# Attention weights stored per head, the seventh block of keys as one full product: 12 products per pair of heads and query range become 11

## The chip, the cores and the metric

The kernel runs on one core of a Trainium2 chip. The metric is the device time of one execution in microseconds. TensorE multiplies matrices, VectorE, ScalarE and GpSimd work on rows of up to 128 partitions, and SyncE issues the transfers (DMAs). In the profile they are PE (with PEld for its weight loads), DVE, ACT, POOL and SP.

## The reference

Two layers follow each other. The inputs are 8 batches, 12 heads, 448 rows and 64 columns per head.

```python
q_n, k_n = (rmsnorm(q, g_q), rmsnorm(k, g_k))
scores = scale * np.matmul(q_n, k_n.transpose(0, 1, 3, 2))
attn = np.exp(scores - np.max(scores, axis=-1, keepdims=True))
attn = attn / (np.sum(attn, axis=-1, keepdims=True) + 1e-09)
x = heads_side_by_side(np.matmul(attn, v))          # (8, 448, 768)
h = gelu(x @ w_in)                                  # (8, 448, 1024)
u, v = h[..., :512], h[..., 512:]
v_n = (v - mu) / np.sqrt(var + 1e-06) * g_ln
v_s = np.einsum('ts,bsd->btd', w_sg, v_n) + b_sg[None, :, None]
out = x + (u * v_s) @ w_out
```

`w_in` and `w_out` are float64 at the kernel's input and are decoded in the kernel.

## The kernel before

**Precision.** Most products are made from 16-bit floats: a number is split into a high part and a low part, and a product of two numbers is high x high + high x low + low x high. So attention times v is three products: `vh` with the high attention weights, `vl` with the high ones, and `vh` with the low ones.

**The work on attention.** A pair is two heads, a unit is two pairs (`NG = 2`); there are 48 pairs and 24 units. The 448 rows are taken as 7 groups of 64 (`C7 = 7`; row number p x 7 + c is place p of group c). For each of the 7 row blocks `t` of a unit, `scores` has 12 products of 64 rows by 64 columns for each of two heads; the output of one head holds 64 queries of each of the two pairs on its 128 partitions, and 448 keys in a row. VectorE takes the maximum (`jk`, `nm`), ScalarE the exponential `ex` with its sum, into 32-bit words `[P, 2, S]`. The 16-bit halves of these words serve as the attention weights: the upper half is the high part, the lower half, scaled by `UNIT`, the low part. They are written to `ahl` by two instructions (`scaled(ahl[:, 0], ...)` on ScalarE, `scaled(ahl[:, 1], ...)` on VectorE or ScalarE), 896 elements each: in `ahl` stand the high parts of head 0, of head 1, then the low parts of head 0, of head 1. One DMA transposes `ahl` in 14 blocks of 128 columns into `at`, so that keys come to the partitions.

448 keys are three and a half blocks of 128. So the fourth block of `at` has the last 64 keys of head 0 on its lower 64 partitions, and the first 64 of head 1 on its upper ones; the same holds for the low parts seven blocks later. v is laid out to match: per pair, `vr` holds for each head three blocks of 128 rows, and one 64-row group of each head shares a block. Four DMAs bring the v rows of three pairs.

```python
steps = [[(lo, CM), (hi, CM)]] + [[(slice(0, P), c), (slice(0, P), C4 + c)] for c in range(CM)]
blocks = [(v_, o, hx) for v_, o in (("vh", 0), ("vl", 0), ("vh", C7)) for hx in steps]
blocks = blocks[0::C4] + [x for m, x in enumerate(blocks) if m % C4]
```

`pv(u, e)` is called twice for a unit: e = 0 for four row blocks (256 columns a matmul), e = 1 for three (192 columns). With `steps` above, each of the three products has one step of 64 rows (`lo` for head 0, `hi` for head 1) and three of 128 rows, and each step is two matmuls, one for each head, side by side on 64 columns of the array each. The 64-row steps of both pairs come first. A call yields after step 5 and step 14 (`CUTS`), so that other work can come between its three pieces. Then VectorE multiplies by `row` (the reciprocal sums), ScalarE makes `xh` and VectorE `xl`, which the second layer (`moe`) reads.

**v.** `vsquares` sums the squares of three pairs' v on ScalarE, from which `vscale` makes one power of two for a batch; `vsplit` makes `vh` (ScalarE) and `vl` (VectorE), 448 elements a partition.

**The order.** Every operation is recorded on a tape with a cost by formula (`Tape.cost`), and `schedule` then writes the order of each engine as a list scheduler does: of what is ready, the lowest program number comes first, and an operation given to `either` goes to the engine that would end it first by the formula. TensorE tries to stay in one mode (128 or 64 rows, 128 or 64 columns), since a change of mode has a cost there. Because all is emitted in one place, nearly all instructions bear the line number L439 in the profile, and one is told from another by the tile names. Pools are rings: `at` has one buffer for each of its two ranges, `ahl` three, `vh` and `vl` four, `vr` two. SyncE issues all DMAs from one queue in the written order.

Of the kernel before, what the change touches and what calls it, by code (L numbers as in the profile page):

```python
# [46 lines left out]
NOT, NX, NEX = 2, 6, 2  # L47
EXP_SET = "natural_log_exp_and_others"
# [55 lines left out]
class Tape:  # L104
# [30 lines left out]
    def cost(self, q, op, a, kw):  # L135
# [15 lines left out]
        if q.eng != "S" and "dma" in op:  # L151
            return 700, 4000, None
# [48 lines left out]
    def record(self, q, op, a, kw):  # L201
# [12 lines left out]
        if q.eng == "S":  # L214
            t.preds |= self.after
# [231 lines left out]
def kernel(  # L447
# [76 lines left out]
    ENG = dict(A=A, V=V, G=G)  # L524

# [54 lines left out]
    def decode(dst, raw, most=None):  # L580
# [8 lines left out]
        V.scalar_tensor_tensor(out=di, in0=lo, scalar=29, in1=di, op0=ALU.logical_shift_right, op1=ALU.bitwise_or)  # L589

    def weights():
# [10 lines left out]
        def load_raw(j):  # L602
            if j < len(chunks):
# [3 lines left out]
                SP.dma_start(out=raws[j].rearrange("p a b -> p (a b)"),  # L607
# [5 lines left out]
        for x in (1, 0):  # L613
# [13 lines left out]
            for t in range(KT):  # L627
                wh, wl = (wi[:, t, x, n] for n in range(2))
                A.activation(out=wh, in_=dec[t], func=AF.Copy, scale=wsc)
                V.scalar_tensor_tensor(out=wl, in0=dec[t], scalar=wsc, in1=wh, op0=ALU.mult, op1=ALU.subtract)  # L630
# [33 lines left out]
        if PADS:  # L664
# [50 lines left out]
    def load_v(i):  # L715
# [6 lines left out]
        vr = ld.tile([P, GV, C7, D], F32, name="vr", bufs=NVR)  # L722
        vp = vr.rearrange("p g c d -> p g (c d)")
        src = v[b, 2 * g:2 * (g + GV)].rearrange("(g h) (p c) d -> h p g (c d)", h=2, c=C7)
        for h, half, s0, c0, n in ((0, lo, 0, 0, C4), (0, hi, 0, C4, CM), (1, lo, C4, C4, CM), (1, hi, CM, 0, C4)):
            SP.dma_start(out=vp[half, :, s0 * D:(s0 + n) * D], in_=src[h][:, :, c0 * D:(c0 + n) * D])
        for j in range(GV):
            VR[i + j] = vp[:, j]
# [48 lines left out]
    def vsquares(i):  # L777
# [6 lines left out]
        n = GV * C7 * D  # L784
# [12 lines left out]
    def vsplit(i):  # L797
        r = R.setdefault(i, {})
        sc = VS[i // NP]["sc"]
        vh, vl = (att.tile([P, C7, D], F16, name="v" + c, bufs=NVH) for c in "hl")  # L800
# [3 lines left out]
        V.scalar_tensor_tensor(out=vl.rearrange("p c d -> p (c d)"), in0=vr, scalar=sc, in1=vf, op0=ALU.mult, op1=ALU.subtract)  # L804
# [4 lines left out]
    def scores(u):  # L809
# [5 lines left out]
        for t in range(C7):  # L815
# [24 lines left out]
            scaled(ahl[:, 0], halves[:, :, :, 1], 1.0, HI)  # L840
            scaled(ahl[:, 1], halves[:, :, :, 0], UNIT, EL)
# [15 lines left out]
    def rows(e, rh, rl):  # L857
# [9 lines left out]
        row = att.tile([P, C4 * P], F32, name="row", bufs=1)[:, 0:n * P]  # L867
# [5 lines left out]
    def pv(u, e):  # L873
# [20 lines left out]
        V.tensor_tensor(out=ps, in0=ps, in1=row, op=ALU.mult)  # L894
# [5 lines left out]
        V.tensor_tensor(out=xl, in0=ps, in1=xh, op=ALU.subtract)  # L900
# [19 lines left out]
    def moe(b, early=False):  # L920
# [49 lines left out]
        def layernorm():  # L970
# [22 lines left out]
            for t in range(CK):  # L993
                s_ = tiles[t][1]
                V.tensor_scalar(out=vg[:, s_], in0=vg[:, s_], scalar1=mv[:, t, 0:1], scalar2=y[:, t:t + 1],
                                op0=ALU.subtract, op1=ALU.mult)
                copy(vh[:, s_], vg[:, s_], VH)
# [40 lines left out]
        for f in range(FT):  # L1038
            ps = ps_m.tile([P, 512], F32, name="ms_", tag="mm")
            n = 0  # L1040
            for t in range(CK):
                p0, p1, o, k = 0, P, t * DH + f * P, t
                if t == CM:
                    p0 = f // 2 * HP
                    p1, o = p0 + HP, t * DH + f % 2 * P
                    if PADS:
                        p0, p1, k = 0, P, CM + f // 2
# [201 lines left out]
```

## Time and profile before

| | |
|---|---|
| runs, us | 858.94, 857.5, 861.17 |
| profiled execution, us | 860.37 |
| its span, us | 858.6 |
| busy TensorE / ScalarE / VectorE / GpSimd, us | 743.0 / 722.3 / 668.2 / 304.5 |
| mean granted TensorE clock | 0.936 |
| matmuls `pv` / `s` | 2304 / 2016 |
| instructions `ahl` on ScalarE / VectorE | 192 / 144 |
| transposing DMAs `at` / `qt` | 168 / 48 |

The busy times are unions over the span. A row of a group gives its line, engine, operation, tiles out<-in, form, count, then busy time and mean duration, then the idle time of the engine before it and what ended that. In a row of the time order the numbers are the start in us and the length from the first start to the last end, xN the number of instructions merged. `64*64` ahead of a matmul's form says that it uses 64 rows and 64 columns of the array.

### The profile page before, as it was taken

What the parts mean: (1) busy time and instruction counts of PE and PEld (TensorE: products, weight loads), DVE (VectorE), ACT (ScalarE), POOL (GpSimd) and SP (SyncE); (2) the same over time, 40 slices, a digit from 0 to 9 for tenths busy, and PEclk for the clock granted to TensorE, in tenths of its full rate; (3) what the DMA queues carried; (4) which work ended last, traced back from release to release, by engine and by line L of the source; (5) the groups of instructions that cost most, each with busy time, mean ns of one, the idle gap of its engine ahead of it and who ended that gap; (6) DMA issues with size and microseconds to landing.
All of it is one profiled execution on the core that took longest, in us unless ns stands there. A gap on an engine that the chain in (4) does not pass through costs nothing.

```text
span 858.6 us, 21024 instructions
## 1 busy us (share of the span) xinstructions
PE 743.0 (87%) x7766; PEld 475.1 (55%) x7766; DVE 668.2 (78%) x1691; ACT 722.3 (84%) x1495; POOL 304.5 (35%) x457
## 2 busy tenths in 40 slices
PE   0445568954999979999999999999999999999997
PEld 0223343532675548655765568556855686558557
DVE  6978988889988878977976898878987978574250
ACT  4677879998898999898989999889999999895451
POOL 2543350045534634452444246323435335000000
PEclk9658668966999999999999999999999999999999
DMA  6999999969999998999699979997999699646002
GB/s 165 252 241 195 216 207 199 213 141 200 169 234 218 226 190 166 246 209 166 137 206 225 226 145 226 240 209 134 198 225 218 140 223 200 136 90 143 19 1 74
DMA packets 433944, 155.97 MB, mean 182 GB/s; under 512 B 402545, under 2 KB 427697, under 8 KB 433841
## 3 DMA queue, kind: packets, MB, share of 16 engines
q1 hardware_dynamic: 433840, 154.63, 89.6%
q8 instruction: 61, 1.00, 0.5%
q14 instruction: 43, 0.34, 0.1%
HBM read 43.57 MB, written 11.01 MB: 64 GB/s over the span
## 4 chain that ended last, share of the span: by engine, by line
PE 55%; ACT 17%; DVE 12%; DMA 9%; issue 5%; POOL 1%; SPq 1%; ACTq 0%; DVEq 0%; POOLq 0%
PE pv L439 11%; PE s L439 7%; DMA at<-ahl 6%; ACT ex L439 4%; ACT ahl L439 3%; DVE jk L439 2%; ACT L439 2%; ACT sqk L439 2%; PE row L439 1%; DVE ahl L439 1%; DMA qk<-in_k_dram 1%; ACT vg L439 1%; ACT u L439 1%; ACT vh L439 1%; DVE pv L439 1%
## 5 line engine op out<-in xcount | busy, mean ns | idle before, releaser
L439 DVE TENSOR_SCALAR_CACHE_REDUCE jk<-s 128x448 bf16<-128x448 f32 x336 | 199.0, 615 | 34.8 <-PE s L439 34.4
L439 ACT ACTIVATE ex<-s,nm 128x448 int32<-128x448 f32 x336 | 213.6, 641 | 12.1 <-DVE jk L439 9.8
L439 ACT ACTIVATE ahl<-ex 128x896 f16<-128x896 uint16 x192 | 181.9, 957 | 9.5 <-DMA at<-ahl 8.9
L439 PE MATMUL s<-qt 64*64 64x448 f16 x2016 | 142.8, 375 | 48.4 <-DMA qt<-hl 21.3
L439 PEld LDWEIGHTS <-vh 128*64 128x64 f16 (+2 forms) x1792 | 103.2, 112 | 103.6 <-issue 55.7
L439 PE MATMUL pv<-at,vh 128*64 128x192 f16 (+3 forms) x1536 | 133.0, 275 | 27.6 <-ACT ex L439 12.3
L439 DVE TENSOR_SCALAR ahl<-ex 128x896 f16<-128x896 uint16 x144 | 102.5, 712 | 28.8 <-ACT ex L439 22.7
L439 PEld LDWEIGHTS <-qt 64*64 64x64 f16 x2016 | 64.7, 110 | 94.4 <-issue 52.5
L439 POOL TENSOR_TENSOR hl<-qk,hl 128x896 f16<-128x896 f32 (+2 forms) x69 | 93.7, 1364 | 41.7 <-ACT hl L439 9.7
L439 PEld LDWEIGHTS <-wi 128*128 128x128 f16 x576 | 54.5, 99 | 55.5 <-issue 7.2
L439 POOL TENSOR_TENSOR qk<-qk,ny 128x896 f32<-128x896 f32 x46 | 77.1, 1690 | 14.5 <-DVE ahl L439 7.5
L439 POOL TENSOR_TENSOR qk<-qk,gg 128x896 f32<-128x896 f32 x23 | 48.1, 2093 | 96.0 <-ACT sqk L439 77.4
L439 PEld LDWEIGHTS <-xh 128*128 128x128 f16 (+1 forms) x648 | 49.7, 102 | 47.7 <-issue 20.8
L439 PE MATMUL pv<-at,vl 128*64 128x192 f16 (+3 forms) x768 | 74.0, 273 | 0.0
L439 ACT ACTIVATION_READ_ACCUMULATOR ex<-s,nm 128x1 f32 x336 | 71.6, 213 | 0.0
L439 POOL TENSOR_SCALAR rx<-sums 128x8 f32<-128x8 f32 (+1 forms) x48 | 15.0, 313 | 141.8 <-ACT ex L439 140.3
L439 PEld LDWEIGHTS <-vl 128*64 128x64 f16 (+2 forms) x896 | 56.1, 114 | 12.8 <-issue 0.7
L439 DVE TENSOR_REDUCE ss<-sqk 128x14 f32<-128x896 f32 x48 | 51.8, 1079 | 10.2 <-ACT sqk L439 10.1
L439 DVE TENSOR_TENSOR pv<-pv,row 128x512 f32<-128x512 f32 (+1 forms) x48 | 30.2, 629 | 34.3 <-PE pv L439 34.1
L439 ACT ACTIVATE sqk<-qk 128x896 f32<-128x896 f32 x48 | 45.8, 960 | 3.4 <-DMA qk<-in_k_dram 1.8
L439 PEld LDWEIGHTS <-xl 128*128 128x128 f16 (+1 forms) x408 | 36.6, 102 | 19.5 <-DVE v_i L439 1.1
L439 ACT ACTIVATE xh<-pv 128x512 f16<-128x512 f32 (+1 forms) x48 | 26.2, 547 | 24.4 <-DVE pv L439 23.7
(1104 smaller groups left out, 1799.7 us busy)
## 6 DMA issues: line engine op xcount, KB each, us to landing
qk<-in_q_dram SPq DMA_DIRECT2D x48, 224.0 KB, 3.9
qk<-in_k_dram SPq DMA_DIRECT2D x48, 224.0 KB, 4.7
out_dram<-ot SPq DMA_DIRECT2D x56, 192.0 KB, 3.4
raw<-in_moe_w_in_dram SPq DMA_DIRECT2D x12, 512.0 KB, 5.4
vr<-in_v_dram SPq DMA_DIRECT2D x32, 192.0 KB, 4.2
vr<-in_v_dram SPq DMA_DIRECT2D x32, 144.0 KB, 3.7
rawo<-in_moe_w_out_dram SPq DMA_DIRECT2D x8, 384.0 KB, 3.6
at<-ahl SPq DMA_TRANSPOSE x168, 4.6
```

What stands on the lines that cost most here:

```text
L439: ins = getattr(q.nc_eng, op)(*first, *a, **kw)
```

## The change

Attention weights are written per head: in `ahl`, and so in `at`, head 0 has its seven blocks, then head 1. Within a head come the 448 high parts, then the low parts of the last 64 keys, then the low parts of the first 384. So the fourth block of a head has the high parts of the last 64 keys on the lower 64 partitions, and their low parts on the upper ones. v's last 64 rows stand twice in `vr`, on the lower and on the upper partitions, so that one product of 128 rows with `vh` gives high x high and high x low for these keys, and one with `vl` gives low x high (and low x low, which was not computed before). A pair has 3 x 3 steps for the first 384 keys and 2 for the last 64: 11, all of 128 rows, in place of 9 of 128 and 3 of 64. `blocks` is now in the order of pair, then product; the cuts stay after steps 5 and 14, of 22 steps in place of 24. The low parts are written by two instructions, of 768 and 128 elements. `vr`, `vh`, `vl` have 512 elements a partition in place of 448; the squares count the last rows twice, in a scale that only has to be some power of two. v is loaded by three DMAs for three pairs.

```diff
-        vr = ld.tile([P, GV, C7, D], F32, name="vr", bufs=NVR)
-        vp = vr.rearrange("p g c d -> p g (c d)")
-        src = v[b, 2 * g:2 * (g + GV)].rearrange("(g h) (p c) d -> h p g (c d)", h=2, c=C7)
-        for h, half, s0, c0, n in ((0, lo, 0, 0, C4), (0, hi, 0, C4, CM), (1, lo, C4, C4, CM), (1, hi, CM, 0, C4)):
-            SP.dma_start(out=vp[half, :, s0 * D:(s0 + n) * D], in_=src[h][:, :, c0 * D:(c0 + n) * D])
+        vr = ld.tile([P, GV, 2 * C4, D], F32, name="vr", bufs=NVR)
+        vp = vr.rearrange("p g (h c) d -> p (g h) (c d)", h=2)
+        src = v[b, 2 * g:2 * (g + GV)].rearrange("h (p c) d -> p h (c d)", c=C7)
+        for half, s0, c0, n in ((lo, 0, 0, C4), (hi, 0, C4, CM), (hi, CM, CM, 1)):
+            LD[VQ].dma_start(out=vp[half, :, s0 * D:(s0 + n) * D], in_=src[:, :, c0 * D:(c0 + n) * D])
...
-        n = GV * C7 * D
+        n = GV * 2 * C4 * D
...
-        vh, vl = (att.tile([P, C7, D], F16, name="v" + c, bufs=NVH) for c in "hl")
+        vh, vl = (att.tile([P, 2 * C4, D], F16, name="v" + c, bufs=NVH) for c in "hl")
...
-            scaled(ahl[:, 0], halves[:, :, :, 1], 1.0, HI)
-            scaled(ahl[:, 1], halves[:, :, :, 0], UNIT, EL)
+            parts = ahl.rearrange("p x h n -> p (x h n)").rearrange("p (h n) -> p h n", h=2)
+            scaled(parts[:, :, 0:S], halves[:, :, :, 1], 1.0, HI)
+            scaled(parts[:, :, CK * P:C7 * P], halves[:, :, 0:SM, 0], UNIT, EL)
+            scaled(parts[:, :, S:CK * P], halves[:, :, SM:S, 0], UNIT, TL)
...
-        steps = [[(lo, CM), (hi, CM)]] + [[(slice(0, P), c), (slice(0, P), C4 + c)] for c in range(CM)]
-        blocks = [(v_, o, hx) for v_, o in (("vh", 0), ("vl", 0), ("vh", C7)) for hx in steps]
-        blocks = blocks[0::C4] + [x for m, x in enumerate(blocks) if m % C4]
+        blocks = [(v_, m, m + o) for v_, o in (("vh", 0), ("vl", 0), ("vh", CK)) for m in range(CM)]
+        blocks += [("vh", CM, CM), ("vl", CM, CM)]
...
-        steps = [(j, x) for part in (blocks[:3], blocks[3:]) for j in range(NG) for x in part]
-        for k_, (j, (v_, o, hx)) in enumerate(steps):
-            for h, (ks, c) in enumerate(hx):
-                mm(out=pc[h * HP:(h + 1) * HP, j], lhsT=R[NG * u + j][v_][ks, c], rhs=av[ks, o + c, j, 0:n],
+        steps = [(j, x) for j in range(NG) for x in blocks]
+        for k_, (j, (v_, m, o)) in enumerate(steps):
+            for h in range(2):
+                mm(out=pc[h * HP:(h + 1) * HP, j], lhsT=R[NG * u + j][v_][:, h * C4 + m], rhs=av[:, h * C7 + o, j, 0:n],
                    start=(k_ == 0), stop=(k_ == len(steps) - 1), skip_group_check=True)
```

`TL` is 'VA' as `EL` is, so VectorE or ScalarE. The rest of the diff adds switches (`STK`, `DEC`, `XL`, `VL`, `WL` and the queues' `RQ` to `XQ`) whose values leave the program as it was: all DMAs stay on SyncE's queue, and the operations on their engines.

On TensorE, here is the start of the first piece of a call with 192 columns near the middle of the program (the tile `at_7512` before, its counterpart `at_7476` now):

```order
L439 MATMUL ms__7767<-ws_h,vl 128x448
L439 LDWEIGHTS vh
L439 MATMUL pv<-at_7512,vh 64x3x64
L439 LDWEIGHTS vh
L439 MATMUL pv<-at_7512,vh 64x3x64
L439 LDWEIGHTS vl
L439 MATMUL pv<-at_7512,vl 64x3x64
```
```order
L443 LDWEIGHTS rl
L443 MATMUL row<-ident_h,rl 64x128
L443 LDWEIGHTS vh
L443 MATMUL pv<-at_7476,vh 64x3x64
L443 LDWEIGHTS vh
L443 MATMUL pv<-at_7476,vh 64x3x64
L443 LDWEIGHTS vh
L443 MATMUL pv<-at_7476,vh 64x3x64
```

Before, this piece is the 64-row steps of both pairs, `vh` and `vl` in turn, and score products in the same mode follow it; now it is the first six 128-row steps of the first pair, and it follows the products of `row`, which have the same mode. The third piece of a call has 14 matmuls in place of 18.

On VectorE, these are the rows ahead of the thirteenth unit's first multiplication by `row`:

```order
L439 SCALAR_TENSOR_TENSOR vl<-vr,v_s,vh 128x448 x2
L439 TENSOR_SCALAR ahl<-ex 128x896
L439 TENSOR_SCALAR jk,nm<-s 128x448 x2
L439 RECIPROCAL ry<-rx 128x6
L439 TENSOR_SCALAR jk,nm<-s 128x448 x2
L439 TENSOR_TENSOR pv<-pv,row 128x512
```
```order
L443 TENSOR_SCALAR ahl<-ex 128x2x384
L443 TENSOR_SCALAR ahl<-ex 128x2x64
L443 RECIPROCAL ry<-rx 128x6
L443 TENSOR_SCALAR ahl<-ex 128x2x384
L443 TENSOR_SCALAR ahl<-ex 128x2x64
L443 TENSOR_TENSOR pv<-pv,row 128x512
```

The one copy of 896 elements has become two, which mostly follow each other, and the maxima (`jk`) of this place now stand elsewhere.

On SyncE's queue, this is the load of v for three pairs, in the second half of the program:

```order
L439 DMA vr<-in_v_dram 64x3x256
L439 DMA vr<-in_v_dram 64x3x192 x2
L439 DMA vr<-in_v_dram 64x3x256
```
```order
L443 DMA vr<-in_v_dram 64x6x256
L443 DMA vr<-in_v_dram 64x6x192
L443 DMA vr<-in_v_dram 64x6x64
```

Four issues have become three, the last of which brings the repeated rows in pieces of 64 numbers.

More of the change, by code (lines that the diff above doesn't have):

```diff
@@ L539, in two, with stt @@
         tape.either(*[(ENG[e], "tensor_tensor", dict(out=out, in0=in0, in1=in1, op=op)) for e in on])
+    def stt(out, in0, by, in1, op0, op1, on):
+        tape.either(*[(ENG[e], "scalar_tensor_tensor", dict(out=out, in0=in0, scalar=by, in1=in1, op0=op0, op1=op1)) for e in on])
     SSW = 2 * C7
@@ L629, in weights @@
                 A.activation(out=wh, in_=dec[t], func=AF.Copy, scale=wsc)
-                V.scalar_tensor_tensor(out=wl, in0=dec[t], scalar=wsc, in1=wh, op0=ALU.mult, op1=ALU.subtract)
+                stt(wl, dec[t], wsc, wh, ALU.mult, ALU.subtract, WL)
                 if t % 2:
@@ L663, in weights @@
             yield
-        if PADS:
+        if PADS and not STK:
             for w_t in (ws_h, ws_l):
@@ L866, in rows @@
             return ps
-        row = att.tile([P, C4 * P], F32, name="row", bufs=1)[:, 0:n * P]
+        row = att.tile([P, C4 * P], F32, name="row", bufs=2 if "G" in XL else 1)[:, 0:n * P]
         scaled(row, ps, 2.0 ** -25, RW)
@@ L893, in pv @@
             row = rows(e, *r_)
-        V.tensor_tensor(out=ps, in0=ps, in1=row, op=ALU.mult)
+        if "G" in XL:
+            sx = att.tile([P, C4 * P], F32, name="sx", tag="row", bufs=2)[:, 0:n * P]
+            V.tensor_tensor(out=sx, in0=ps, in1=row, op=ALU.mult)
+            ps = sx
+        else:
+            V.tensor_tensor(out=ps, in0=ps, in1=row, op=ALU.mult)
         if e == 0:
@@ L899, in pv @@
         copy(xh, ps, XH)
-        V.tensor_tensor(out=xl, in0=ps, in1=xh, op=ALU.subtract)
+        two(xl, ps, xh, ALU.subtract, XL)
         if e == 1:
@@ L992, in layernorm @@
             vl = mlp.tile([P, CM * DH + FH], F16, name="vl")
-            for t in range(CK):
+            for t in (CM, *range(CM)) if STK else range(CK):
                 s_ = tiles[t][1]
@@ L996, in layernorm @@
                                 op0=ALU.subtract, op1=ALU.mult)
+                if STK and t == CM:
+                    vs = mlp.tile([P, 2, FH], F16, name="vs")
+                    for x, (own, far) in enumerate(((lo, hi), (hi, lo))):
+                        copy(vs[own, x], vg[own, s_], VH)
+                        V.tensor_tensor(out=vl[own, s_], in0=vg[own, s_], in1=vs[own, x], op=ALU.subtract)
+                        SP.dma_start(out=vs[far, x], in_=vl[own, s_])
+                    V2["vs"] = vs
+                    continue
                 copy(vh[:, s_], vg[:, s_], VH)
@@ L1047, in moe @@
                         p0, p1, k = 0, P, CM + f // 2
+                if STK and t == CM:
+                    for wx in (ws_h, ws_l):
+                        mm(out=ps[:, 0:S], lhsT=V2["vs"][:, f // 2, f % 2 * P:(f % 2 + 1) * P], rhs=wx[:, CM], start=False, stop=(wx is ws_l))
+                    continue
                 for vx, wx in ((vh, ws_h), (vh, ws_l), (vl, ws_h)):
```

25 lines of the change are left out of this document (15 added, 10 removed).

## The prediction

> **What bounds the kernel now.** I read the windows by stage first, then the chain of waits by stage, then single rows. The times of the runs are 857.5 to 861.17 with the median 858.94; the profiled execution took 860.37, of which the span below is the part that the engines show, with 1.8 us around it.
>
> ```profile
> span 858.6 us, 21024 instructions
> ```
> ```profile
> core 0: us, PE busy (x) PEld busy (x) DVE busy (x) ACT busy (x) POOL busy (x), PEclk, DMA share, GB/s
> 0.00:240.00 240.00, 140.59 (x1440) 82.74 (x1440) 205.59 (x506) 193.35 (x384) 92.07 (x133) 0.78 0.95 201
> 240.00:780.00 540.00, 528.47 (x5759) 340.33 (x5758) 442.17 (x1137) 497.50 (x1057) 210.43 (x317) 1.00 0.98 192
> 780.00:859.00 79.00, 73.94 (x570) 52.06 (x569) 20.39 (x48) 31.48 (x56) 2.02 (x8) 0.99 0.23 53
> ```
> ```profile
> 660.00:720.00 60.00, 59.47 (x660) 42.97 (x659) 49.38 (x131) 56.93 (x125) 27.12 (x40) 1.00 0.91 180
> ```
>
> There are three stages. Up to 240 us the weights are decoded and TensorE has a granted clock of 0.78 and much idle time; VectorE is the fullest engine (205.59 of 240, 86%). From 240 to 780 TensorE is busy for 98% at the full clock, with ScalarE close behind (497.50 of 540, 92.1%) and VectorE at 82%. After 780 TensorE is nearly alone. The 60 us from 660 show that ScalarE can be at 94.9% (56.93 of 60) while TensorE still runs through.
>
> ```profile
> by line: DMA at<-ahl 13.2%; PE pv L439 10.4%; issue 8.4%; ACT ahl L439 7.6%; ACT ex L439 5.6%; DMA qk<-in_k_dram 4.0%; DVE jk L439 3.5%; ACT sqk L439 3.5%; DVE dec L439 3.1%; SPq L439 2.8%; ACT L439 2.7%; DMA qt<-hl 2.6%; PE s L439 2.5%; AC
> ...
> by line: PE pv L439 12.4%; PE s L439 9.8%; DMA at<-ahl 4.2%; issue 4.0%; ACT ex L439 4.0%; ACT L439 2.1%; ACT ahl L439 2.1%; PE row L439 1.8%; DVE jk L439 1.8%; DVE ahl L439 1.5%; ACT vg L439 1.4%; ACT u L439 1.1%; ACT vh L439 1.0%; ACT sqk
> ...
> by line: PE pv L439 6.6%; PE mv__13219 L439 5.2%; PE mv__13214 L439 5.1%; PE mv__13351 L439 5.1%; PE mu__13423 L439 4.3%; PE mu__13363 L439 4.3%; PE mu__13454 L439 4.3%; PE mu__13398 L439 4.3%; PE mo__13710 L439 3.5%; PE mo__13154 L439 3.4%
> ```
>
> These are the chains of the three stages in order. The products of attention with v (`pv`) are on the chain for 10.4% of 240, 12.4% of 540 and 6.6% of 79 us: 25.0 + 67.0 + 5.2 = 97.2 us. The instructions that make `ahl` are on it too: on ScalarE for 7.6% of 240 and 2.1% of 540, 29.5 us; on VectorE for 1.5% of 540, 8.1 us. The change makes the first cheaper and the second dearer.
>
> **TensorE.** A call of `pv` had 12 steps for each of 2 pairs, each step one matmul for either head; now it has 11. So 24 steps become 22, and the removed ones are of the 64-row kind: 6 of these go and 4 whole ones come. What matters is whether a 64-row step costs less than a whole one.
>
> ```profile
> 588.94 0.33 PE L439 MATMUL pv<-at,vh 64*64 64x192 f16 x4
> 589.10 0.24 PE L439 MATMUL pv<-at,vl 64*64 64x192 f16 x2
> 589.18 0.25 PE L439 MATMUL pv<-at,vh 64*64 64x192 f16 x2
> 589.36 0.36 PE L439 MATMUL ms__9495<-ws_h,vh 128*128 128x448 f16 x1
> ```
> ```profile
> 645.03 0.41 PE L439 MATMUL pv<-at,vl 128*64 128x192 f16 x6
> 645.27 0.41 PE L439 MATMUL pv<-at,vh 128*64 128x192 f16 x6
> ```
> ```profile
> 542.85 0.38 PE L439 MATMUL pv<-at,vh 64*64 64x256 f16 x4
> 543.07 0.27 PE L439 MATMUL pv<-at,vl 64*64 64x256 f16 x2
> ```
> ```profile
> 750.35 0.49 PE L439 MATMUL pv<-at,vl 128*64 128x256 f16 x6
> 750.68 0.49 PE L439 MATMUL pv<-at,vh 128*64 128x256 f16 x6
> ```
>
> From start to start, 4 matmuls of 64 rows take 0.16 us at 192 columns and 0.22 at 256, that is 0.08 and 0.11 for a step of two; 6 whole ones take 0.24 and 0.33, again 0.08 and 0.11. A half product costs as much as a whole one. The saving is two steps in a call: 2 x 0.11 + 2 x 0.08 = 0.38 us for the two calls of a unit, 9.1 us for 24 units at full clock, 6.8 for the 18 between 240 and 780. On the chain it is 1/12 of 97.2, **8.1 us**, and that is my term: 2.1 + 5.6 + 0.4 by stage.
>
> [...]
>
> A change of mode: 589.18 to 589.36 is 0.18 us where 0.08 was due, 0.10 for the change. The first six steps of a call could stand inside a run of score products in their own mode and no longer can, but the last two pieces always needed a change; over the whole written order I count 363 changes before and 367 now. That is 0.4 us, put at nothing.
>
> **The weights' copies.** For each of 168 row blocks ScalarE and VectorE copy the high and low halves of `ex` into `ahl`. Two instructions of 896 elements become three: 896 (the high halves, ScalarE), 768 and 128 (the low ones). In the new order the 768 stand on ScalarE 19 times and on VectorE 149 (before 24 and 144), the 128 on ScalarE 53 times and on VectorE 115.
>
> ```profile
> L439 ACT ACTIVATE ahl<-ex 128x896 f16<-128x896 uint16 x192 | 181.9, 957 | 9.5 <-DMA at<-ahl 8.9
> L439 DVE TENSOR_SCALAR ahl<-ex 128x896 f16<-128x896 uint16 x144 | 102.5, 712 | 28.8 <-ACT ex L439 22.7 <-DMA at<-ahl 5.5
> L439 ACT ACTIVATE row<-row 128x512 f32<-128x512 f32 x24 | 14.4, 600 | 2.0 <-PE row L439 2.0
> L439 ACT ACTIVATE row<-row 128x384 f32<-128x384 f32 x24 | 11.7, 488 | 0.0
> L439 ACT ACTIVATE ny<-nt 128x28 f32<-128x28 f32 x24 | 5.7, 237 | 0.2
> L439 DVE COPY xt<-xl 128x64 f16<-128x64 f16 x24 | 5.8, 243 | 0.0
> L439 ACT ACTIVATE vh<-vr,v_s 128x448 f16<-128x448 f32 x48 | 32.4, 676 | 7.1 <-PE pv L439 5.5 <-DVE v_s L439 1.4
> L439 DVE SCALAR_TENSOR_TENSOR vl<-vr,v_s,vh 128x448 f16<-128x448 f32 x48 | 36.1, 754 | 4.6 <-ACT vh L439 4.3
> L439 ACT ACTIVATE sqv<-vr 128x1344 bf16<-128x1344 f32 x16 | 21.4, 1337 | 3.2 <-issue 2.5 <-DMA vr<-in_v_dram 0.7
> ```
> ```profile
> L439 DVE TENSOR_SCALAR ahl<-ex x144: 593/624/2401, 30.1 to 786.1; 128x896 f16<-128x896 uint16 x144
> ```
>
> ScalarE: the two rows of `row` give 112 ns for 128 elements. 168 x 957 + 19 x (957 - 112 = 845) + 53 x 300 ns is 160.8 + 16.1 + 15.9 = 192.8 us against 192 x 957 = 183.7: **+9.1**. The 300 lie between 237 (28 elements) and 488 (384), nearer the first; the ends give +5.8 and +19.1. VectorE: the least time, 593 for 896 elements, and the 243 of a 64-element copy bracket the small one; a slope of 0.55 ns per element (from the least 593 down to that copy's least of 130 in its tile's rows below) gives 243 + 35 = 278 ns for 128 and 712 - 71 = 641 for 768. So 149 x 641 + 115 x 278 = 95.5 + 32.0 against 102.5: **+25.0**. With 130 to 712 for the small one it is +8 to +75. That two runs of 384 keep the rate of one run of 896 isn't shown for `ahl`; the copies of `hl`, which are cut in runs as well, have a least time of 346 for their smallest form of 384 elements, on the same slope.
>
> ```profile
> L439 DVE COPY xt<-xl x24: 130/174/1130, 136.8 to 722.1; 128x64 f16<-128x64 f16 x24
> ```
> ```profile
> L439 DVE CAST hl<-qk x33: 346/620/2097, 26.5 to 658.9; 128x384 f16<-128x384 f32 x14, 128x512 f16<-128x512 f32 x10, 128x896 f16<-128x896 f32 x9
> ```
>
> [...]
>
> v: its rows of a pair grow from 448 to 512 elements. `vh` adds at most 14% of 32.4, `vl` of 36.1, `sqv` of 21.4 (4.6, 5.1, 3.1), and with a fixed part as in `row` some 2.7, 3 and 2.7. Three copies of `hl` of 512 elements went from ScalarE to VectorE, at 600 ns as in `row` 1.8 us. Together ScalarE has +12.7 us and VectorE +30.
>
> ```profile
> core 0: us, DVE busy (x) ACT busy (x), PEclk, DMA share, GB/s
> 240.00:780.00 540.00, 82.18 (x118) 126.49 (x132) 1.00 0.98 192
> ```
>
> This window view of `ahl` alone has 250 of 336 instructions in the long stage, 74%: there ScalarE gets +9.4 (506.9) and VectorE +22 (464, 86%). VectorE's part has cover: it was idle for 98 us there, and 641 + 278 = 919 ns on VectorE lie beside the 957 of ScalarE's high half, so a block whose parts start together isn't later. Scaled by the shares on the chain, ScalarE's `ahl` adds 5% of 29.5 = 1.5 and VectorE's 24% of 8.1 = 2.0, of which I keep half for that cover. For v I add 0.7:
>
> ```profile
> vr<-in_v_dram SPq DMA_DIRECT2D x32, 192.0 KB, 4.2
> vr<-in_v_dram SPq DMA_DIRECT2D x32, 144.0 KB, 3.7
> ...
> qt<-hl SPq DMA_TRANSPOSE x48, 4.4
> ```
>
> a load of 672 KB in four DMAs becomes 768 KB in three; 14% of the 4.2 to landing is 0.6, once where a load is late, the rest is loaded one batch ahead. SP's queue gets 16 issues fewer, and the transposes behind them stay as many and as large; each waits for three copies now.
>
> Sum: -8.1 + 1.5 + 1.0 + 0.7 = **-4.9 us**, 855.5 against this execution, **854.0 against the median**. With nothing hidden the additions on the chain are 4.2 and it is -3.9; with all hidden -8.1.
>
> **Rivals**, in terms of the median. *ScalarE becomes the bound* (slower): at its present share of 92.1% its 506.9 us need 550 us in the long stage, 10 more, and with 0.4 gained at the end the time is 868.5; at the best stretch's 94.9% they need 534, 6 less, which is the forecast's gain. It decides from 506.9 / 540 = 93.9%: if ScalarE can't be held above that, the change loses. For it: the ScalarE instructions come in an order that waits for VectorE's maxima; against: the stretch at 660. *The additions take back what TensorE gives* (no difference): if the small copy on VectorE costs as much as the large one does on average, 712, VectorE's term on the chain is 73% of 8.1 = 5.9 and the sum is 0: about 859. *The half products were half price after all*: 12 steps were worth 10.5, 11 are 5% more, +4.6 + 3.2 and 867; the rows speak against it.
>
> **How the numbers follow.** Forecast 0.62, ScalarE as the bound 0.20, no difference 0.15, half price 0.03. The whole order is written anew, and waits shift both ways; I take a third of the 4.0% of 540 that the chain calls issue, 7 us, for that. The range begins at 854 - 3.2 (all additions hidden) - 7 = 843 and ends at 867, with the half-price case, short of ScalarE's full 868.5; about one case in ten is left out above and one below. Half a per cent, 4.3 us, is what a measurement tells from no change; the forecast lies just beyond it, so of its 0.62 I count 0.45 as faster and 0.17 as the same. The same has 0.17 + 0.15 + 0.03 (a mild case of ScalarE) = 0.35, slower 0.17 + 0.03 = 0.20.
>
> **What would show it.** In the changed profile: 2112 `pv` matmuls, all 128*64, at 0.08 and 0.11 a step; the 128-element `ahl` near 280 ns on VectorE and 300 on ScalarE, the 768 near 640; ScalarE busy about 735 us in all; the `pv` share of the chain down by 8. If instead the stage from 240 is as long as before with idle TensorE ended by ScalarE or by the transposes, the first rival is right. The forecast is wrong if the small copies cost 0.5 us or more, or if runs of 384 lose VectorE's rate.

## The result, and the profile after

The changed kernel takes **871.39 us** (median of 6 runs, 868.0 to 875.2) against 859.64 us (857.5 to 862.03) for the kernel before, measured beside it: a ratio of 1.0138, with a 95% interval of 1.0103 to 1.0173. It is slower by 11.8 us, where 4.9 us less were forecast and the range ended at 867. Three executions of the runs below that took 1266.1, 1456.9 and 3938.7 us are left out of every median and ratio.

```profile
span 868.9 us, 20822 instructions
```

The windows of the changed kernel by the same three stages:

```profile
core 0: us, PE busy (x) PEld busy (x) DVE busy (x) ACT busy (x) POOL busy (x), PEclk, DMA share, GB/s
0.00:240.00 240.00, 139.27 (x1425) 82.33 (x1426) 210.56 (x545) 200.53 (x416) 96.96 (x138) 0.81 1.00 212
240.00:780.00 540.00, 511.65 (x5470) 320.81 (x5469) 442.24 (x1192) 490.08 (x1048) 210.69 (x308) 1.00 0.97 187
780.00:869.00 89.00, 84.21 (x683) 59.72 (x680) 30.61 (x78) 41.36 (x79) 2.54 (x11) 1.00 0.26 63
```

TensorE has less to do (735.1 us in all, 743.0 before), but between 240 and 780 us it is idle for 28.4 us (540 less 511.65) where it was for 11.5 (540 less 528.47), and more is left for later: 84.21 us in the last window against 73.94. ScalarE isn't fuller: 490.08 of 540 us, 90.8% against 92.1%. VectorE has the same 442 us as before. Of the engines that compute, none has taken TensorE's place as the fullest of this stage. The DMA engines show a higher share than TensorE's 94.8%, 0.97 now and 0.98 before. That share alone is no sign of the loss: from 240 us to the end the changed kernel has 0.87 as given, and with set a below it has 0.92 there and takes 860.0 us. No run takes load off the DMA engines.

The groups by form for the operations that the change made or lengthened; the last numbers are the busy time and the mean in ns, then the idle time ahead of them:

```profile
L443 ACT ACTIVATE ahl<-ex 128x896 f16<-128x896 uint16 x168 | 160.5, 957 | 5.3 <-DMA at<-ahl 5.1
...
L443 DVE TENSOR_SCALAR ahl<-ex 128x768 f16<-128x768 uint16 x149 | 97.1, 652 | 28.7 <-ACT ex L443 21.9 <-DMA at<-ahl 5.3 <-ACT row L443 0.8
...
L443 DVE SCALAR_TENSOR_TENSOR vl<-vr,v_s,vh 128x512 f16<-128x512 f32 x48 | 41.4, 864 | 5.9 <-ACT vh L443 5.9
...
L443 ACT ACTIVATE vh<-vr,v_s 128x512 f16<-128x512 f32 x48 | 34.9, 726 | 6.8 <-DVE v_s L443 3.7 <-PE pv L443 3.0
L443 DVE TENSOR_SCALAR ahl<-ex 128x128 f16<-128x128 uint16 x115 | 29.6, 257 | 2.2 <-DMA at<-ahl 2.2
...
L443 ACT ACTIVATE sqv<-vr 128x1536 bf16<-128x1536 f32 x16 | 23.9, 1493 | 2.1 <-issue 1.3 <-DMA vr<-in_v_dram 0.8
...
L443 ACT ACTIVATE ahl<-ex 128x128 f16<-128x128 uint16 x53 | 16.3, 307 | 0.4
L443 ACT ACTIVATE ahl<-ex 128x768 f16<-128x768 uint16 x19 | 16.0, 843 | 3.5 <-DMA at<-ahl 3.3
```

And products of attention with v, in the order of time:

```profile
642.24 0.63 PE L443 MATMUL pv<-at,vh 128*64 128x256 f16 x8
642.71 0.28 PE L443 MATMUL pv<-at,vl 128*64 128x256 f16 x2
642.81 0.49 PE L443 MATMUL pv<-at,vh 128*64 128x256 f16 x6
643.14 0.28 PE L443 MATMUL pv<-at,vl 128*64 128x256 f16 x2
```
```profile
549.52 0.52 PE L443 MATMUL pv<-at,vh 128*64 128x256 f16 x6 [1.21 <-DMA at<-ahl]
549.87 0.49 PE L443 MATMUL pv<-at,vl 128*64 128x256 f16 x6
```
```profile
650.14 0.44 PE L443 MATMUL pv<-at,vh 128*64 128x192 f16 x6
650.41 0.41 PE L443 MATMUL pv<-at,vl 128*64 128x192 f16 x6
```

All products use 128 rows. At 256 columns a step of two takes 0.10 us from start to start (642.71 to 642.81), and three steps 0.33 (642.81 to 643.14) to 0.35 us (549.52 to 549.87, behind a wait for a transposing DMA). At 192 columns three steps take 0.27 us here (650.14 to 650.41) and 0.24 in another place (593.49 to 593.73). So a step costs about what it cost. The copies cost about what was forecast (below). The prices of single operations thus explain nothing of the loss.

The chain of waits in the long stage:

```profile
by line: DMA at<-ahl 8.5%; PE pv L443 8.3%; issue 7.5%; PE s L443 6.3%; ACT ex L443 4.2%; POOL qk L443 3.3%; ACT L443 3.2%; ACT ahl L443 3.1%; DVE jk L443 2.8%; DVE ahl L443 2.0%; ACT vg L443 1.9%; PE row L443 1.7%; ACT u L443 1.5%; DVE hl 
```

The products' share fell from 12.4% to 8.3%, but the transposing DMAs of the weights rose from 4.2% to 8.5% and "issue" from 4.0% to 7.5%. The chain is more often outside TensorE. What TensorE itself waited for from 240 us to the end, longest in total first (total, times, longest), of the kernel before:

```profile
engine line waited for: us in total, times, longest us
PE ms__4409 L439 <- DVE xl L439: 4.8, 1, 4.8
PE pv L439 <- DMA at<-ahl: 1.1, 2, 0.6
PE s L439 <- ACT row L439: 1.1, 1, 1.1
```

and of the changed kernel:

```profile
PE pv L443 <- DMA at<-ahl: 6.2, 5, 2.7
PE pv L443 <- ACT ex L443: 2.6, 2, 1.9
PE row L443 <- DVE xl L443: 2.5, 2, 2.2
PE ms__4477 L443 <- ACT ex L443: 2.4, 1, 2.4
PE mo__7985 L443 <- DVE gtl L443: 1.8, 1, 1.8
```

There is no single new wait. The largest row, the transposes of the weights, has grown by 5.1 us and stands for five places. Summed over all rows of this view, ScalarE ended 12.7 us of TensorE's idle time where it ended 2.6, VectorE 8.6 for 6.7, and the transposes 6.2 for 1.1.

The loss builds up slowly. The first multiplication by `row` on VectorE in a unit starts, in the changed kernel and the kernel before, at 197.56 and 215.24 us in the fifth unit, 243.59 and 244.12 in the sixth, 368.62 and 366.60 in the tenth, 584.62 and 579.53 in the seventeenth, 803.35 and 792.83 in the last. A lead of 17.7 us is nearly gone one unit later, and from the tenth unit on the changed kernel is behind. Such a picture calls for the question of whether the work or its order did it.

### The profile page after: what moved, and what is told of

The parts are those of the page before. It is cut to its first block, busy times and chain, and to the rows that moved or that the text cites. A ratio compares the mean times of both kernels' runs of the same rounds, so it can differ in the third digit from the quotient of the medians.

```text
span 868.9 us, 20822 instructions
## 1 busy us (share of the span) xinstructions
PE 735.1 (85%) x7574; PEld 462.9 (53%) x7574; DVE 683.4 (79%) x1814; ACT 732.0 (84%) x1540; POOL 310.2 (36%) x457
## 4 chain that ended last, share of the span: by engine, by line
PE 41%; ACT 15%; DVE 9%; DMA 6%; issue 6%; POOL 4%; SPq 0%; POOLq 0%; ACTq 0%; DVEq 0%
PE pv L443 7%; DMA at<-ahl 5%; PE s L443 4%; ACT ex L443 4%; ACT ahl L443 2%; ACT L443 2%; POOL qk L443 2%; DVE jk L443 2%; PE row L443 1%; DVE ahl L443 1%; ACT u L443 1%; ACT vg L443 1%; DMA vr<-in_v_dram 1%; ACT sqk L443 1%; DVE vl L443 1%
## 5 line engine op out<-in xcount | busy, mean ns | idle before, releaser
L443 ACT ACTIVATE ahl<-ex 128x896 f16<-128x896 uint16 (+2 forms) x240 | 186.2, 804 | 9.2 <-DMA at<-ahl 8.4
L443 PE MATMUL s<-qt 64*64 64x448 f16 x2016 | 133.7, 377 | 54.7 <-DMA qt<-hl 28.1
L443 DVE TENSOR_SCALAR ahl<-ex 128x768 f16<-128x768 uint16 (+1 forms) x264 | 118.9, 480 | 30.9 <-ACT ex L443 21.9
L443 PEld LDWEIGHTS <-vh 128*64 128x64 f16 (+1 forms) x1600 | 93.0, 113 | 85.9 <-issue 38.9
L443 PE MATMUL pv<-at,vh 128*64 128x256 f16 (+1 forms) x1344 | 102.9, 276 | 28.6 <-DMA at<-ahl 25.3
L443 PEld LDWEIGHTS <-qt 64*64 64x64 f16 x2016 | 54.6, 110 | 109.1 <-issue 57.8
L443 POOL TENSOR_SCALAR rx<-sums 128x8 f32<-128x8 f32 (+1 forms) x48 | 21.2, 442 | 192.7 <-ACT ex L443 191.3
L443 PE MATMUL pv<-at,vl 128*64 128x256 f16 (+1 forms) x768 | 81.2, 275 | 0.0
L443 PEld LDWEIGHTS <-xh 128*128 128x128 f16 (+1 forms) x648 | 50.1, 102 | 49.8 <-issue 24.2
L443 PEld LDWEIGHTS <-vl 128*64 128x64 f16 (+1 forms) x896 | 55.0, 114 | 27.0 <-issue 11.7
L443 DVE TENSOR_TENSOR pv<-pv,row 128x512 f32<-128x512 f32 (+1 forms) x48 | 30.2, 628 | 27.2 <-PE pv L443 27.0
L443 PE MATMUL row<-ident_h,rh 128*64 128x128 f16 x336 | 27.0, 232 | 25.0 <-POOL rh L443 19.0
```

Of the source, the lines that this page charges most:

```text
L443: ins = getattr(q.nc_eng, op)(*first, *a, **kw)
```

## The experiments

Three theories were tested. **A**: the third copy per row block, or ScalarE's added work in general, is on the path. **B**: the 22 whole products in their new places cost TensorE time that the 24 did not. **C**: the planner writes the whole program's order anew from costs and due times, any such new order moves the time by about as much as was seen, and the changed work itself costs little. The ratio of each run is against the kernel before, run beside it on the same chip; the medians of that kernel were 861.17 to 862.01 us there. A ratio is the better comparison between two runs of this list.

### Taking the third copy away, and adding it to the kernel before

The changed kernel with its low parts in one copy of 896 elements:

```diff
-            scaled(parts[:, :, CK * P:C7 * P], halves[:, :, 0:SM, 0], UNIT, EL)
-            scaled(parts[:, :, S:CK * P], halves[:, :, SM:S, 0], UNIT, TL)
+            scaled(parts[:, :, S:C7 * P], halves[:, :, :, 0], UNIT, EL)
```


> The changed kernel with the low parts of ahl written by one instruction of 896 elements in their natural order (so low parts meet the wrong rows of v; nothing else is left out). Theory A, the third copy: its 16 us on ScalarE and 30 us on VectorE are what lengthens the program, so without it the time falls from 871 to 850-857, below the kernel before by TensorE's saving. Theory B, the products: eleven whole steps in one order fit worse between the score products, so the time stays at 867-873. Theory C, the written order: a schedule written anew comes out better or worse by about 1% whatever is in it, so anything from 855 to 875 without regard to the copy.

Measured: 866.36 us, 1.008 [1.0053, 1.0107]. And the kernel before with the third copy:

```diff
-            scaled(ahl[:, 1], halves[:, :, :, 0], UNIT, EL)
+            scaled(ahl[:, 1, :, 0:SM], halves[:, :, 0:SM, 0], UNIT, EL)
+            scaled(ahl[:, 1, :, SM:S], halves[:, :, SM:S, 0], UNIT, EL)
```


> The kernel before with only the low parts' copy cut into 768 and 128 elements; products and v as before. Theory A: 859 plus 8 to 12, 867-872. Theory B: 859 within 0.5%. Theory C: anywhere within 1% of 859 to 862.

Measured: 859.53 us, 0.9978 [0.9961, 0.9995]. The groups by form of this kernel show that it does have the same added instructions:

```profile
L439 DVE TENSOR_SCALAR ahl<-ex 128x768 f16<-128x768 uint16 x144 | 91.3, 634 | 31.8 <-ACT ex L439 29.8 <-DMA at<-ahl 1.3
...
L439 DVE TENSOR_SCALAR ahl<-ex 128x128 f16<-128x128 uint16 x116 | 30.2, 260 | 0.0
...
L439 ACT ACTIVATE ahl<-ex 128x128 f16<-128x128 uint16 x52 | 16.2, 311 | 0.3
```

The kernel before takes 168 more copies and isn't slower. So the third copy isn't a cost that shows wherever it is put. Either run also has a new order, so neither is the price of the copy alone, and what the first of them gained by taking it away can't be laid to that price.

### The third copy on other engines

```diff
-TL = 'VA'
+TL = 'V'
```


> The changed kernel with all 168 small copies on VectorE. ScalarE loses 53 x 0.307 = 16 us, VectorE gets 53 x 0.257 = 14. Theory A in the form that ScalarE's idle time stays: 871 - 12 = 857-861. Theory A in the form that VectorE's or the block's latency counts: 871-880. Theory B: 871.

Measured: 863.61 us, 1.0031 [1.0012, 1.0051]. VectorE gets all 168 small copies, and the kernel is 8 us faster than as given. With `TL = 'G'`, on GpSimd:

> The changed kernel with all 168 small copies on GpSimd, which is busy for 36%: ScalarE loses 16 us, VectorE 30, GpSimd gets 168 x about 0.55 = 90. Theory A: 850-860, as with two copies, unless GpSimd's lateness delays the transposes, then 865-880. Theory B: 871.

Measured: 873.8 us, 1.0148 [1.0133, 1.0164]. In the groups by form the small copy costs 675 ns there; the 0.55 us expected was the author's estimate, which no run shows:

```profile
L443 POOL TENSOR_SCALAR ahl<-ex 128x128 f16<-128x128 uint16 x168 | 113.4, 675 | 262.0 <-DVE ahl L443 102.4 <-ACT ex L443 95.4 <-DMA at<-ahl 14.0
```

GpSimd is busy for 416.5 us instead of 310.2 and the time is that of the changed kernel as given. ScalarE has 722.7 us of work with the copy on VectorE and 726.8 with it on GpSimd, against 732.0. The first run fits A, if ScalarE were the path; the second does so only if GpSimd's slower copy took the gain away. The next pair tests the path.

### Less work for ScalarE

The squares of v that set its scale are taken of one pair in three, in the changed kernel

```diff
-        n = GV * 2 * C4 * D
+        n = 2 * C4 * D
```


> The changed kernel with the squares of v summed over one pair of three only (the scale comes out as another power of two): ScalarE has 16 x about 1.0 = 16 us less to do, spread over the program. Theory A2, ScalarE is the bound and its idle time (136 us in the kernel before, 137 in the changed one) is a constant of the program: 871 - 14 to 16 = 855-858. Theory C, the written order decides: 858-875, without regard to ScalarE's work.

and, with `n = C7 * D` for `n = GV * C7 * D`, in the kernel before:

> The same cut of 16 us of ScalarE's work in the kernel before. Theory A2: 860 - 14 = 845-848. If TensorE is the bound from 240 us on, as the forecast had it: 857-862. Theory C: 853-868.

Measured: 878.31 us, 1.0208 [1.0149, 1.0266] for the changed kernel, and 854.18 us, 0.9923 [0.9901, 0.9944] for the kernel before. In the groups of the first the squares fell from 23.9 to 10.2 us, and the planner, which gives a copy to the engine that it thinks is free, moved 11 large copies to ScalarE (30 instead of 19):

```profile
L443 ACT ACTIVATE ahl<-ex 128x768 f16<-128x768 uint16 x30 | 25.1, 836 | 2.1 <-DMA at<-ahl 1.9
...
L443 ACT ACTIVATE sqv<-vr 128x512 bf16<-128x512 f32 x16 | 10.2, 635 | 3.8 <-issue 2.9 <-DMA vr<-in_v_dram 0.9
```

The busy times on the page of this run, and on the page of a run that follows below (the changed kernel with set b):

```profile
PE 738.2 (84%) x7574; PEld 465.3 (53%) x7574; DVE 664.1 (76%) x1797; ACT 729.3 (83%) x1557; POOL 308.2 (35%) x457
```
```profile
PE 736.8 (86%) x7574; PEld 464.5 (54%) x7574; DVE 674.8 (78%) x1798; ACT 737.6 (86%) x1556; POOL 308.0 (36%) x457
```

In the kernel before, ScalarE's work fell from 722.3 to 706.5 us and the kernel became faster, as A says. In the changed kernel only 2.7 us came off (729.3 against 732.0), because of the moved copies, and VectorE has 19 us less (664.1 against 683.4); yet the kernel is slower, by 0.7% of the kernel before, which the intervals of the two ratios hardly tell from nothing. So this pair doesn't settle A. The second line does more: with set b ScalarE has 737.6 us of work, 5.6 more than in the order as given, and the changed kernel takes 862.9 us. Together the two lines contradict A in the form that more work on ScalarE is more time. And a change that has nothing to do with the products moved the time of the kernel before by 0.8%, more than was forecast for the change under study.

### The same work in another order

So the order alone was changed, with the same work. The planner also chooses the engine of some copies, so a few of them change sides: ScalarE has 1484 to 1496 instructions in seven orders of the kernel before and 1525 to 1556 in seven of the changed one. `HYST` is how far ahead of its due time the planner lets a matmul go to stay in the array's mode (a change of mode showed 0.10 us in the kernel before, 589.18 to 589.36 us with 0.08 due):

```diff
-SWITCH, HYST = (133, 92), 160
+SWITCH, HYST = (133, 92), 140
```


> The changed kernel with one number of the list scheduler altered (it may put off a change of TensorE's mode for 140 program numbers in place of 160). The same work, another order. Theory A2: 871 within 0.3%, apart from what moves between ScalarE and VectorE. Theory C: anywhere from 858 to 878, several us away from 871.

> The same alteration (140 in place of 160) in the kernel before. Theory A2: 860 within 0.3%. Theory C, in the form that the kernel before owes its time to an order that was chosen among many: 863-875, never faster than 860 by more than 0.3%.

Measured: 867.97 us, 1.0079 [1.005, 1.0108] for the changed kernel, 868.92 us, 1.0089 [1.0064, 1.0113] for the kernel before. With the allowance that the planner adds between a result and TensorE's start on it (`START`, 70 for 60):

```diff
-START = dict(T=60, A=34, V=33, G=85, S=28, N=0)
+START = dict(T=70, A=34, V=33, G=85, S=28, N=0)
```


> The changed kernel, written in another order: the list scheduler's allowance between a result and TensorE's start is 70 in place of 60. The same work. Theory C1 (the change costs nothing by itself, and its 1.4% is that the order of the kernel before was a good one and the order of the changed kernel is not): over several such pairs the changed kernel and the kernel before differ by less than 0.4% in the mean. Theory C2 (the change costs some 4 to 9 us whatever the order): the changed kernel is behind by 0.5 to 1% in the mean. Alone: 864-873 by C2, 860-868 by C1.

> The kernel before with the same alteration (70 in place of 60). C1: 860-868, as far from 860 as its twin e9 was. C2: 857-864, several us less than e10.

Measured: 866.71 us, 1.0066 [1.004, 1.0092], and 867.37 us, 1.0062 [1.0036, 1.0089]. With the offset of the due times of the second layer's work:

```diff
-MOFF, MOFF0, GP = 300, 100, 350
+MOFF, MOFF0, GP = 275, 100, 350
```


> The changed kernel with the second layer's work put off by 275 program numbers in place of 300. The same work in another order. C1: 860-868; C2: 864-873.

> The kernel before with the same alteration (275 in place of 300). C1: 860-868; C2: 857-864, several us less than e12.

Measured: 863.15 us, 1.0025 [1.0008, 1.0042], and 867.38 us, 1.0069 [1.0051, 1.0087].

Three times the kernel before loses 0.6 to 0.9% by a new order of the same work, and is then not measurably faster than the changed kernel in that order. The order of the kernel before as given is better than these three neighbours; that of the changed kernel as given is worse than its own. With `HYST` at 140 the kernel before is late at the end as the changed one is. These are the last unit's first multiplications by `row`, of the kernel before as given, with 140, and of the changed kernel as given:

```profile
792.83 0.70 DVE L439 TENSOR_TENSOR pv<-pv,row 128x512 f32<-128x512 f32 x1 [5.82 <-PE pv L439]
```
```profile
799.29 0.70 DVE L439 TENSOR_TENSOR pv<-pv,row 128x512 f32<-128x512 f32 x1 [2.88 <-PE pv L439]
```
```profile
803.35 0.70 DVE L443 TENSOR_TENSOR pv<-pv,row 128x512 f32<-128x512 f32 x1 [4.14 <-PE pv L443]
```

The waits that ScalarE ends come with it too: 10.4 us of TensorE's idle time from 240 us on, against 2.6 in the order as given and 12.7 in the changed kernel.

Two further sets of constants lie farther off. Set a was chosen because the planner's own forecast for the changed kernel was shortest with it, set b for the kernel before; both were given to both kernels. Set a:

```diff
-BIAS = dict(A=0, V=0, G=0)
+BIAS = dict(A=100, V=0, G=150)
-CA = 200
+CA = 160
-AG = 85
-OVER, PATIENCE = dict(V=130, G=150), 300
-START = dict(T=60, A=34, V=33, G=85, S=28, N=0)
+AG = 110
+OVER, PATIENCE = dict(V=150, G=130), 400
+START = dict(T=70, A=44, V=38, G=85, S=28, N=0)
...
```


> The changed kernel, same work, with a second set of the planner's constants (BIAS, CA, AG, OVER, PATIENCE, START and M1), chosen because the planner's own forecast of the changed kernel was shortest with it. Theory: the order written decides, and the changed kernel is no slower in itself. Then it stands below its shipped order (1.0138) by 5 to 15 us, 856 to 866 us. Rival: the changed work itself costs 5 us or more; then it stays at 866 or above in this order too, and the kernel before is at least 5 us faster with the same constants.

> The kernel before, same work, with the constants of the run above, which were not chosen for it. Theory: within 1% of the run above, of either sign, 860 to 870 us. Rival (the changed work costs 5 us or more): at least 5 us faster than the run above.

Measured: 859.95 us, 0.9988 [0.9966, 1.0011] for the changed kernel; 861.61 us, 1.0008 [0.9992, 1.0024] for the kernel before. Set b:

```diff
-CUTS = (5,14)
-CA = 200
-CV = 70
+CUTS = (2, 13)
+CA = 180
+CV = 60
-BIAS = dict(A=0, V=0, G=0)
+BIAS = dict(A=50, V=150, G=150)
-OVER, PATIENCE = dict(V=130, G=150), 300
-START = dict(T=60, A=34, V=33, G=85, S=28, N=0)
+OVER, PATIENCE = dict(V=130, G=170), 400
+START = dict(T=60, A=34, V=33, G=80, S=33, N=0)
...
```


> The changed kernel, same work, with a third set of constants, chosen because the planner's forecast of the kernel before was shortest with it. Theory: 858 to 872 us, and within 1% of the kernel before in the same constants. Rival (the changed work costs 5 us or more): at least 5 us slower than the kernel before with them.

> The kernel before, same work, with the third set of constants, chosen by the planner's forecast for this kernel. Theory: 852 to 866 us; its own shipped order at 860 is among its better ones, so at most 8 us below it. Rival (the changed work costs 5 us or more): at least 5 us below the run above.

Measured: 862.86 us, 1.0023 [1.0005, 1.0041] for the changed kernel; **850.62 us, 0.9886 [0.986, 0.9912]** for the kernel before, the fastest of all runs and faster than both kernels as given. The last two runs asked whether a chosen set always does that: a second set chosen for the changed kernel, and a second one for the kernel before, each found apart from the first:

```diff
-SC, SV = 7, 4
+SC, SV = 7, 5
-SWITCH, HYST = (133, 92), 160
+SWITCH, HYST = (133, 92), 150
-CA = 200
+CA = 180
-AG = 85
+AG = 110
...
```


> The changed kernel, same work, with a fourth set of constants, chosen for the changed kernel by the planner's forecast in a search that had nothing to do with the one of the second set. If its good orders are as good as those of the kernel before, one of two chosen sets should come near 851 us; if the change costs it some 9 us at its best, this one too stays at 857 to 866 us, as the second set did (860.0).


```diff
-MOFF, MOFF0, GP = 300, 100, 350
+MOFF, MOFF0, GP = 300, 100, 450
-SWITCH, HYST = (133, 92), 160
-BIAS = dict(A=0, V=0, G=0)
+SWITCH, HYST = (133, 92), 120
+BIAS = dict(A=100, V=100, G=0)
...
```


> The kernel before, same work, with a fifth set, chosen for the kernel before in a search that had nothing to do with the one of the third set (850.6). If a choice by the planner's forecast brings the kernel before a gain on the chip, 848 to 856 us; if the third set was a lucky one, 857 to 866 us.

Measured: 860.81 us, 0.9996 [0.9971, 1.002] for the changed kernel, and 859.93 us, 0.9977 [0.9949, 1.0005] for the kernel before. Neither comes near the 850.6, so choosing by the planner's forecast doesn't bring such a gain each time, and why set b brought it isn't known. No order of the changed kernel that was tried came below 859.95 us.

### What the pairs say together

Six orders were run with both kernels. The view by windows, from 240 us to the end of the span, shows what TensorE did. For the order as given, the kernel before and then the changed one:

```profile
240.00:858.60 618.60, 602.41 (x6328) 392.39 (x6326) 462.56 (x1185) 528.98 (x1112) 212.44 (x325) 1.00 0.88 174
```
```profile
240.00:868.90 628.90, 595.86 (x6151) 380.52 (x6149) 472.85 (x1269) 531.45 (x1126) 213.24 (x319) 1.00 0.87 170
```

with `HYST` at 140, `START` at 70 and `MOFF` at 275, each time the kernel before and then the changed one:

```profile
240.00:867.20 627.20, 605.85 (x6352) 392.29 (x6350) 463.38 (x1192) 528.47 (x1110) 221.26 (x325) 1.00 0.86 172
```
```profile
240.00:865.70 625.70, 600.73 (x6134) 381.46 (x6132) 465.89 (x1267) 533.32 (x1127) 212.65 (x319) 0.99 0.86 170
```
```profile
240.00:865.60 625.60, 602.86 (x6316) 394.76 (x6310) 466.48 (x1189) 526.67 (x1103) 212.17 (x324) 0.99 0.85 172
```
```profile
240.00:861.50 621.50, 596.07 (x6141) 379.44 (x6140) 474.62 (x1283) 531.00 (x1130) 214.66 (x322) 1.00 0.87 173
```
```profile
240.00:866.00 626.00, 602.95 (x6320) 393.05 (x6316) 460.55 (x1184) 530.81 (x1111) 215.74 (x324) 0.99 0.86 172
```
```profile
240.00:860.80 620.80, 596.48 (x6149) 381.16 (x6148) 468.02 (x1276) 526.52 (x1118) 213.16 (x319) 0.99 0.89 172
```

with set a, the kernel before and then the changed one:

```profile
240.00:860.60 620.60, 603.63 (x6343) 392.85 (x6341) 467.58 (x1198) 522.90 (x1097) 212.17 (x322) 0.99 0.88 172
```
```profile
240.00:858.00 618.00, 597.11 (x6209) 383.53 (x6208) 477.66 (x1295) 534.88 (x1138) 212.30 (x322) 1.00 0.92 175
```

and with set b:

```profile
240.00:847.30 607.30, 595.97 (x6278) 390.00 (x6276) 453.54 (x1174) 519.08 (x1091) 213.10 (x319) 1.00 0.88 174
```
```profile
240.00:860.40 620.40, 595.25 (x6118) 381.95 (x6117) 463.15 (x1265) 533.77 (x1134) 212.64 (x319) 1.00 0.90 173
```

The window's length less the busy time of TensorE (the first two numbers) is its idle time. So for all six, in us, with the difference of the two ratios given above, in per cent:

| order | TensorE busy from 240: before, changed | idle: before, changed | changed less before, time |
|---|---|---|---|
| as given | 602.4, 595.9 | 16.2, 33.0 | +1.38% |
| HYST 140 | 605.9, 600.7 | 21.4, 25.0 | -0.10% |
| START 70 | 602.9, 596.1 | 22.7, 25.4 | +0.04% |
| MOFF 275 | 603.0, 596.5 | 23.0, 24.3 | -0.44% |
| set a | 603.6, 597.1 | 17.0, 20.9 | -0.20% |
| set b | 596.0, 595.2 | 11.3, 25.1 | +1.37% |
| mean of differences | -5.4 | +7.0 | +0.34% |

In this window TensorE has less work in every pair, and in every pair it is idle for longer: by 1.3 to 3.9 us in four, by 16.8 and 13.8 us where the kernel before has one of its two best orders among these six. Each row is one execution of either kernel (with `START` at 70 the changed one's was a quick one, 863.25 us against a median of 866.71), and the window starts at a time, not at a point of the program. So the single figures are rough: with set b TensorE has only 0.7 us less in the window, while in the order as given the products of attention with v keep it busy for 146.9 us before and 135.2 now over the whole program.

The mean difference in time, +0.34%, has a 95% interval of about -0.5 to +1.2%, from the scatter of the six (0.82%, divided by the root of 6, times 2.57). The six orders are no random sample: the first was there when the loss was seen, three lie near it, and two were chosen by the planner's forecast. So the interval is a rough guide. What the changed work costs or brings by itself doesn't stand out from what the order does, and the forecast's -0.6% lies just outside the interval. The rival that the changed work costs 5 us in any order fails in four pairs. Not tested is a weaker one, that the change spoils the best orders: the fastest of seven is 850.6 us for the kernel before and 860.0 for the changed one.

## Why the prediction was wrong

**The products: right.** Forecast were 2112 matmuls of 128 rows, 0.08 and 0.11 us a step, and 6.8 us less between 240 and 780 at full clock. Measured are 0.08 to 0.09 and 0.10 to 0.12 us a step, and 0.7 to 6.8 us less from 240 us on, 6.5 us in the order as given. B finds nothing here: the products cost no more. The rival of half products at half price is out.

**The copies: right in size.** Forecast and measured means: 278 and 257 ns for 128 elements on VectorE, 300 and 307 on ScalarE, 641 and 652 for 768 on VectorE, 845 and 843 on ScalarE. The sum for `ahl` is the forecast's 192.8 us on ScalarE (160.5 + 16.3 + 16.0) and 126.7 us on VectorE (97.1 + 29.6) for 127.5. So summing by the rows of the profile held in size. For v, `vh` and the squares cost 2.4 (48 x 50 ns) and 2.5 us more (16 x 156), as forecast, `vl` 5.3 (48 x 110) instead of 3. ScalarE has 9.7 us more in all (732.0 against 722.3) where 12.7 were forecast, VectorE 15.2 (683.4 against 668.2) where 30 were. VectorE's rows for `ahl` and `vl` do grow by 24.2 and 5.3 us; its busy time grows by less because other rows fell, by some 5 us in all, and because time in which instructions overlap counts once: the rows of VectorE by form add up to 765.0 us before and 789.6 now.

**v's loads: underrated, without weight that the runs show.** To landing they took, by the DMA issues of the changed kernel:

```profile
vr<-in_v_dram SPq DMA_DIRECT2D x16, 384.0 KB, 5.5
vr<-in_v_dram SPq DMA_DIRECT2D x16, 288.0 KB, 5.8
...
vr<-in_v_dram SPq DMA_DIRECT2D x16, 96.0 KB, 5.4
```

That is up to 5.8 us against the 4.2 and 3.7 before; 0.6 us more was the forecast. The small load takes 5.4 us too, but the three are issued one right behind the other (at 226.89 us, for example, all three within 1.97 us), so its time to landing isn't its size alone. On the chain of waits such a load stands twice in the changed kernel,

```profile
228.23 4.83 DMA vr<-in_v_dram
```

and 4.47 us at 681.49; in the kernel before it stands there once, 4.82 us at 509.57. (The chain of the changed kernel reaches back to 157 us only, so its first stage can't be compared with that of the kernel before.) The wait at 228 us lies where most of the early lead was lost, between the fifth unit and the sixth; that it cost the lead isn't shown.

**What failed** is the step in which the sum was laid on the old order: "The whole order is written anew, and waits shift both ways; I take a third of the 4.0% of 540 that the chain calls issue, 7 us, for that." The terms were taken from the chain of one order and applied to another order, and the 7 us for that were guessed from a row that has nothing to do with it. In place of 7 us the runs show this: the kernel before, with the same work in seven orders, took 850.6 to 868.9 us, 18 us from end to end, and the changed kernel 860.0 to 871.4. The order as given is better than its three near neighbours for the kernel before, and worse than all six others for the changed one. The same two kernels are within 0.5% of each other in four orders of six. So the first half of C is shown: the order alone moves the time by as much as was seen. Its second half, that the changed work itself costs little, stays open: by the mean of the pairs about 1.0 of the 1.38% is the draw of the order, but the rough interval of that mean allows anything from 0.2% to all of it. Five of the seven orders of the changed kernel lie inside the range of the forecast, none at the 854 us forecast.

A second step failed by less: the gain of TensorE was kept and the additions were given 3.2 us on the chain. Over the pairs, as the mean of the table, TensorE's 5.4 us come back as 7.0 us of idle time. The rival *the additions take back what TensorE gives*, at 859 us, fits four of the six orders by its outcome, but not by its condition: it asked for a small copy of 712 ns on VectorE, and that copy takes 257. Which of the additions makes the idle time (the third copy, which each transposing DMA now waits for too, v's longer rows, or its loads), or whether they do, isn't shown: no run takes one of them out without writing a new order. v's doubled rows alone weren't tried.

**The rival of ScalarE as the bound** had 868.5 us, close to 871.4, and for the wrong reason. Its sign, idle TensorE ended by ScalarE or by the transposes, is there: 12.7 and 6.2 us of the 33.0. But the kernel before shows 10.4 us of the first with `HYST` at 140, without the changed work. And ScalarE isn't held at a ceiling: with set a the changed kernel keeps it busy for 534.88 of 618.0 us, 86.5%, more than the 85.5% (528.98 of 618.6) of the kernel before, and takes 860.0 us; with set b it has 5.6 us more work than in the order as given (737.6 against 732.0), and the kernel takes 862.9 us for 871.4. A time that fits is no evidence for its mechanism.

## What to carry to other kernels

Where a planner or a scheduler writes the order of all engines, a change of the work is also a draw of a new order; before a small difference is laid to the work, move a constant that changes only the order, in both kernels, and see how far the time goes. Forecast such a change with the spread between orders as its uncertainty, and ask how good the present order is among others: here a new order made the kernel before slower three times in six and clearly faster once, while the changed kernel, whose given order was its worst, gained by all six. Relieving an engine that was busy for 98% (528.47 of 540 us) didn't bring what its work fell by: here 5.4 us less of work came back as 7.0 us of idle time, in the mean of six orders. So read how its idle time changes together with its work.

## What was unexpected in the hardware

A third copy per row block, 168 instructions and 46.4 us of engine time (30.2 + 16.2, against some 12 us saved on the large copies), cost the kernel before nothing that could be measured in the one order in which it was tried (0.9978). A load of v with 96 KB took as long to land (5.4 us) as one with 384 KB (5.5 us), issued right behind two larger ones. GpSimd took 675 ns for a copy of 128 elements that took VectorE 257 and ScalarE 307.
